# A four-block attention kernel: masked keys written by transfers, feature-major keys with DMA transposes, the causal triangle on VectorE, half-height numerators and a new instruction order

## The chip, the core and the metric

The kernel runs on one core of a Trainium2 chip. Five engines work side by side, each through its own instructions in order: TensorE (PE, matmuls; its weight loads are listed as PEld), VectorE (DVE), ScalarE (ACT), GpSimd (POOL) and SyncE (SP), which here issues nearly all transfers. Transfers themselves run on 16 DMA engines. The metric is the device time of one execution in microseconds; the kernel before takes 500.85 us (median of three runs, 499.58 to 501.59).

## The reference

Input is x of 2048 tokens by 512 features in bf16. Four blocks follow one another, A, B, A, B, with the same weights; each adds its result to x. There are 32 heads of 16 features.

```python
# block A, for each of 4 segments of 512 tokens
logits = einsum('bhqd,bhkd->bhqk', qs, ks) * scale + mask       # causal inside the segment
p = softmax(logits); a_dot = einsum('bhqk,bhkd->bhqd', p, vs)
pq = phi(qs)                                                    # t + 1 if t > 0, else exp(t)
a_mem = einsum('bhld,bhde->bhle', pq, M) / (einsum('bhld,bhd->bhl', pq, z) + 1e-06)
o = g * a_mem + (1.0 - g) * a_dot
M = M + einsum('bhld,bhle->bhde', phi(ks), vs);  z = z + sum over l of phi(ks)

# block B
pq = q @ w_phi;  pk = k @ w_phi                                 # per head
phi_q = concat(softmax(pq), softmax(-pq));  phi_k = concat(softmax(pk), softmax(-pk))
kv = einsum('bhsf,bhsd->bhfd', phi_k, v);  z = sum over s of phi_k
o = (phi_q @ kv) / (phi_q @ z + 1e-6)
```

Each block begins with a layer norm and ends with a projection `wo`.

## The kernel before, in words

All of x stays in on-chip memory as 16 tiles of 128 tokens. "Layer" 0 and 1 are the two pairs (A, B). Block A of a layer has 4 segments of 4 tiles; a segment's heads go in 4 groups of 8 heads (128 features).

- `a_proj(L, s)` projects a segment: per group the keys K, feature-major (features on partitions), are evacuated to `KT`; four DVE instructions (lines 641 to 645, `Km`) multiply it by a 0/1 column of `m4` into the masked key tile `KM` (pool `pQ`, six buffers), in which each score matmul finds the keys of one head with the other heads' rows at zero. Queries go to `QT`, values to `VT`, and `VS` is a copy with the halves of the partitions swapped, made by two SP transfers. `phi` makes the memory features; those of the keys are transposed by a DMA transpose and summed into `MS32`/`MSb`.
- `a_att(L, s, i)` is one tile of queries. For each group and each key tile j up to i, 8 score matmuls of 64 rows (two at a time, on the two halves of the array) fill one of two 1024-wide PSUM buffers `D`; ACT takes the exponential (1024 elements, or 768 for the diagonal tile, which goes to the pool `pE`); then small matmuls multiply the exponentials with `VT` and `VS` into two PSUM tiles. On the diagonal two more matmuls (`tri` and `two64`, lines 734 to 737) add -1e9 above the diagonal before the exponential. For s >= 1, lines 773 to 796 add the memory term tile by tile: five small matmuls for the denominators (`NMd`), a DVE reciprocal of 32, four matmuls for the numerators (`NM`), a DVE product and a DVE sum. `out_proj` transposes the result, projects it and adds it to x.
- `b_keys(L, c, parts)` handles one 512-token chunk of block B's keys, token-major: per tile a projection, two exponentials on ACT, two DVE sums over heads (line 887, `Zred`), a DVE reciprocal of 64 (line 895, `rZ`), the value projection scaled by it (line 869, `Vt`), and then 8 x 4 matmuls that sum keys times values (`KV`).
- `b_query(L, c)` projects queries, takes exponentials, gets the normalising sums with small matmuls (`Zq`), computes two weights, and per tile runs 8 matmuls of 128 x 128 (`N`, line 952) against the block-diagonal `Rkv`, a copy on ACT, a weighting on DVE, a sum and `out_proj`.

Nothing of the order of the work is decided at run time. Every operation is recorded in a graph with its dependencies; the string `ORDER` then gives, packed, the global sequence of the operations, the engine of each operation that can run on more than one, and the buffer of each tile. `place` reads it; `emit` writes each engine's instructions in that sequence and adds the semaphore waits. So the PE, ACT, DVE and SP queues interleave the stages in a fixed way: projections of segment s+1, keys of block B and attention of segment s are woven together. All matmuls through the helper `mm` carry line 325, exponentials line 331, evacuations line 339 (ACT) or 340 (DVE), transposes line 344.

Of the kernel before, what the change touches and what calls it, by code (L numbers as in the profile page):

```python
# [10 lines left out]
ALU = mybir.AluOpType  # L11
# [285 lines left out]
class Kernel:  # L297
# [78 lines left out]
    def alloc(self):  # L376
# [8 lines left out]
        self.eps32 = sb("eps32", [128, H], BF16)  # L385
        self.two64 = sb("two64", [128, 2, 64], BF16)
        self.tri = sb("tri", [128, 64], BF16)
        self.ones8 = sb("ones8", [128, 8], F32)
# [23 lines left out]
        self.pQ = pool("pQ", N_KM, [128, 4, 2, 2, 128], BF16, {}, ("KM",))  # L412
# [20 lines left out]
    def setup(self):  # L433
# [36 lines left out]
        for g in range(NG):  # L470
            load(lambda g=g: [(self.WB["o"][:, g, :], inp["B_wo"][g * 128:(g + 1) * 128, :].rearrange("(h d) o -> d h o", d=16))],
                 128, [R("WBo", g)])
# [18 lines left out]
        for hf in range(2):  # L491
            v(lambda e, hf=hf: e.tensor_copy(self.tri[64 * hf:64 * hf + 64, :], tw.t[64 * hf:64 * hf + 64, 64 * hf:64 * hf + 64]), 100,
              [tw], [R("tri", hf)])
        v(lambda e: e.memset(self.epsln[:], LN_EPS), 70, [], [R("epsln")])
        v(lambda e: e.memset(self.onesb[:], 1.0), 100, [], [R("onesb")])
        v(lambda e: e.memset(self.eps32[:], 1e-6 / 128.0), 80, [], [R("eps8")])
# [94 lines left out]
    def phi(self, ps, dst, src=None):  # L591
# [4 lines left out]
        if src is None:  # L596
            self.g.op({"dve": (602, lambda e: e.tensor_scalar(dst.t[:], ps.t[:, 0:512], 0.0, None, op0=ALU.max)),
                       "act": (478, lambda e: e.activation(dst.t[:], ps.t[:, 0:512], ACT.Relu))}, [ps[0]], [dst], label="phmax")
        else:
            v(lambda e: e.tensor_scalar(dst.t[:], src.t[:], 0.0, None, op0=ALU.max), 202, [src], [dst], label="phmax", port=True)  # L600
# [23 lines left out]
    def a_proj(self, L, s):  # L624
# [7 lines left out]
        for g in range(NG):  # L632
# [3 lines left out]
            KT = self.T(self.p1, "KT")  # L636
            KM = self.T(self.pQ, "KM")
            pk = self.T(self.p1, "phiKT") if s < 3 else None
            self.wproj(ps, 0, self.WA["k"], [R("WA", "k", g // 2)], g, xT, opens=[KT] + ([pk] if pk else []), label="K")
            self.evac(lambda KT=KT: KT.t[:], lambda ps=ps: ps.t[:, 0:512], 512, [ps[0]], [KT], label="Kev")  # L640
            for sl in range(4):
                fn = lambda e, KM=KM, KT=KT, sl=sl: e.tensor_scalar(  # L642
# [505 lines left out]
```

## Time and profile before

| | before |
|---|---|
| median of three runs | 500.85 us |
| lowest, highest | 499.58, 501.59 us |
| span of the profiled execution | 497.1 us |
| PE, DVE, ACT busy share | 94%, 88%, 89% |
| TensorE clock granted | 9 tenths or more in all 40 slices |
| transfers | 30.20 MB in 89377 packets |

The profile is of one execution; its own time is listed only as the span, from the first to the last instruction. Rows of the profile name the source line, the engine, the operation, the output and input tiles without buffer numbers, the shapes and the count; then busy time and mean duration of one instruction, then idle time of that engine just before and what ended it. Rows of the timeline begin with start and duration in us. Where an instruction overlaps the next, its duration is longer than the distance between the two starts.

### The profile page before, as it was taken

How to read it: one execution, taken by the hardware profiler on the slowest of the kernel's cores; microseconds unless marked ns; L12 is line 12 of the kernel's file. 1: busy time of each engine (PE TensorE's matmuls, PEld its weight loads, DVE VectorE, ACT ScalarE, POOL GpSimd, SP SyncE). 2: the span in 40 equal slices, each digit the busy share in tenths (PEclk: the TensorE clock that was granted, in tenths of full speed). 3: DMA queues.
4: the chain of work that ended last, by engine and by line, in shares of the span. 5: the costliest groups of instructions: out<-in, count | busy, mean ns of one | idle time of the engine just before them, and what ended most of it. 6: DMA issues, size and time to landing. Idle time of an engine off the chain costs nothing.

```text
span 497.1 us, 22749 instructions
## 1 busy us (share of the span) xinstructions
PE 469.4 (94%) x10186; PEld 299.8 (60%) x10282; DVE 438.1 (88%) x1115; ACT 440.9 (89%) x611; POOL 58.8 (12%) x142
## 2 busy tenths in 40 slices
PE   9989999999999989999999999999999999999896
PEld 4446665566676676557555665467566757656652
DVE  7989999998778969987999999999797899889885
ACT  3889999997999989489999999999999998966992
POOL 4512201000001101001220221010001011010000
PEclk9999999999999999999999999999999999999999
DMA  8986733211112031000243444321303112110155
GB/s 227 251 142 89 81 76 47 61 27 38 41 31 53 7 47 36 12 1 1 45 75 74 82 79 69 63 47 34 58 11 50 37 34 34 26 24 2 44 113 164
DMA packets 89377, 30.20 MB, mean 61 GB/s; under 512 B 75936, under 2 KB 89280, under 8 KB 89280
## 3 DMA queue, kind: packets, MB, share of 16 engines
q1 hardware_dynamic: 88928, 28.46, 30.2%
q8 instruction: 80, 1.31, 1.1%
q10 hardware_dynamic: 288, 0.26, 0.2%
q14 instruction: 17, 0.14, 0.1%
q0 software_dynamic: 64, 0.02, 0.1%
HBM read 6.32 MB, written 2.10 MB: 17 GB/s over the span
## 4 chain that ended last, share of the span: by engine, by line
PE 61%; ACT 24%; DVE 9%; issue 3%; DMA 2%; SPq 0%; POOL 0%
PE G L325 41%; PE D L325 18%; ACT p L331 16%; ACT pE L331 6%; DMA X<-in_A_x_dram 1%; DVE p L961 1%; DVE X L826 1%; DVE pS L887 1%; DMA pX<-p 1%; DVE stats L552 1%; PE G L808 1%; DVE WA_v L508 1%; DVE pQ L642 1%; DVE pT L869 0%; ACT WB_v L339 0%
## 5 line engine op out<-in xcount | busy, mean ns | idle before, releaser
L331 ACT ACTIVATE p<-D 128x1024 bf16<-128x1024 f32 x256 | 255.6, 1045 | 13.6 <-PE D L325 12.4
L325 PE MATMUL D<-pK,pQ 64*128 64x128 bf16 (+1 forms) x2560 | 112.3, 212 | 2.9 <-ACT pE L331 0.7
L331 ACT ACTIVATE pE<-D 128x768 bf16<-128x768 f32 x128 | 104.0, 840 | 9.8 <-PE D L325 9.0
L325 PEld LDWEIGHTS D<-pK,pQ 64*128 64x128 bf16 x2560 | 70.9, 94 | 54.9 <-ACT p L331 20.5
L325 PE MATMUL G<-pV,p 64*128 64x34 bf16 (+1 forms) x1632 | 78.9, 178 | 0.5 <-ACT pE L331 0.2
L331 ACT ACTIVATE p<-G 128x512 bf16<-128x512 f32 x112 | 69.0, 633 | 7.8 <-PE G L325 7.0
L325 PEld LDWEIGHTS G<-pV,p 64*128 64x128 bf16 (+1 forms) x1632 | 70.4, 93 | 7.3 <-issue 2.6
L325 PE MATMUL G<-pV,pE 64*128 64x34 bf16 x1024 | 73.0, 175 | 1.5 <-issue 1.5
L325 PE MATMUL G<-pW,pE 64*128 64x34 bf16 x1024 | 71.3, 175 | 0.6 <-issue 0.5
L325 PE MATMUL G<-pW,p 64*128 64x34 bf16 x1536 | 70.4, 176 | 0.8 <-issue 0.8
L325 PEld LDWEIGHTS G<-pW,p 64*128 64x128 bf16 x1536 | 63.8, 93 | 0.8 <-issue 0.4
L560 POOL TENSOR_SCALAR rstd<-mv 128x1 f32<-128x1 f32 x60 | 15.5, 261 | 379.6 <-DVE mv L553 379.6
L325 PEld LDWEIGHTS G<-pV,pE 64*128 64x128 bf16 x1024 | 53.3, 93 | 3.3 <-issue 3.2
L325 PEld LDWEIGHTS G<-pW,pE 64*128 64x128 bf16 x1024 | 50.5, 92 | 0.7 <-issue 0.7
L552 DVE BATCH_NORM_STATS2 stats<-X 128x6 f32<-128x512 bf16 x64 | 43.3, 682 | 3.1 <-DMA X<-in_A_x_dram 2.5
L642 DVE TENSOR_SCALAR pQ<-p,m 128x512 bf16<-128x512 bf16 x128 | 40.8, 340 | 2.6 <-PE D L325 1.6
L887 DVE TENSOR_REDUCE pS<-p 128x32 f32<-128x512 bf16 x64 | 41.7, 671 | 0.9 <-ACT p L331 0.6
L826 DVE TENSOR_TENSOR X<-X,G 128x512 bf16<-128x512 bf16 x48 | 32.5, 682 | 10.6 <-PE G L325 10.2
L869 DVE TENSOR_TENSOR pT<-G,pT 128x1024 bf16<-128x1024 f32 x30 | 36.2, 1212 | 2.3 <-PE G L325 1.9
L562 POOL TENSOR_TENSOR rstd<-rstd,mhalf 128x1 f32<-128x1 f32 x60 | 36.0, 605 | 3.7
L325 PE MATMUL D<-tri,two 64*128 64x256 bf16 x256 | 35.1, 270 | 0.0
L325 PE MATMUL G<-WA_v,pX 128*128 128x512 bf16 x128 | 32.9, 381 | 0.6 <-DVE WA_v L508 0.5
(118 smaller groups left out, 839.6 us busy)
## 6 DMA issues: line engine op xcount, KB each, us to landing
pW<-pV SPq DMA_DIRECT2D x16, 136.0 KB, 3.2
out_dram<-X SPq DMA_DIRECT2D x16, 128.0 KB, 1.8
X<-in_A_x_dram SPq DMA_DIRECT2D x3, 512.0 KB, 7.4
pX<-in_B_wqkv_dram SPq DMA_DIRECT2D x3, 512.0 KB, 7.3
p<-p SPq DMA_TRANSPOSE x76, 2.5
pX<-p SPq DMA_TRANSPOSE x54, 2.5
WA_k<-in_A_wk_dram SPq DMA_DIRECT2D x2, 256.0 KB, 7.5
WA_v<-in_A_wv_dram SPq DMA_DIRECT2D x1, 512.0 KB, 8.4
```

Source lines behind the costliest of these rows:

```text
L325: ins = e.matmul(out_ap, lhsT, rhs, start=st, stop=sp, tile_position=(basep(lhsT), basep(out_ap)))
L331: return self.g.op({"act": (dur, lambda e: e.activation(out_ap(), in_ap(), func, scale=scale))}, reads, writes, opens, label=label)
L508: fn = lambda e, dt=dt: e.tensor_tensor(self.WA["v"][:, dt, :].rearrange("p (h d) -> p h d", h=H), self.WA["v"][:, dt, :].rearrange("p (h ...
L552: v(lambda e: e.bn_stats(self.stats[:, t, :], self.X[:, t, :]), 602, [R("X", t)], [R("st", t)], label="bn")
L560: v(lambda e: e.tensor_scalar(rs, self.mv[:, t, 1:2], LN_EPS, None, op0=ALU.add), 170, [R("mv", t)], [R("rstd", t)], eng="pool", label="rstd")
L562: v(lambda e: e.tensor_tensor(rs, rs, self.mhalf[:], ALU.pow), 540, [R("rstd", t), R("mhalf")], [R("rstd", t)], eng="pool", label="rstd")
L642: fn = lambda e, KM=KM, KT=KT, sl=sl: e.tensor_scalar(KM.t[:, :, sl % 2, :, 64 * (sl // 2):64 * (sl // 2) + 64], KT.t[:].rearrange("p (j h ...
L808: ins = e.matmul(tp.t[:, k * 128:(k + 1) * 128], pair.t[:, sgn * 512 + k * 128:sgn * 512 + (k + 1) * 128], self.ident[:], start=sgn == 0, ...
L826: self.v(lambda e: e.tensor_tensor(self.X[:, t, :], self.X[:, t, :], ps.t[:, 0:512], ALU.add), 602, [R("X", t), ps[0]], [R("X", t)], label ...
L869: v(lambda e: e.tensor_tensor(dst(), ps.t[:, None, 0:512].to_broadcast([128, 2, 512]).rearrange("p s (g d h) -> p s g d h", g=NG, h=8), rz ...
L887: fn = lambda e, sgn=sgn, E=E, Z=Z: e.tensor_reduce(Z.t[:, sgn * 32:(sgn + 1) * 32], E.t[:, sgn * 512:(sgn + 1) * 512].rearrange("p (h d) ...
L961: v(lambda e, Ns=Ns, Tm=Tm, w=w, shape=shape: e.tensor_tensor(shape(Tm.t[:]), shape(Ns.t[:]), w(), ALU.mult), 600, [Ns, AB[0], AB[1]], [Tm ...
```

## The change

The changed kernel makes seven edits.

1. Masked keys: in segments 1 to 3 of both layers, the four DVE multiplications per group give way to transfers on SP that copy only the non-zero rows of `KT` into `KM`. Two groups share one `KT` and one `KM` tile (three buffers of double size in place of six); a pair takes four operations of two DMA copies each. A GpSimd memset zeroes one buffer at the start; the other two get their zeros from the first segment's multiplications, which remain there.
2. Causal triangle: the two `tri` matmuls stay only for the four tiles of layer 0, segment 0; in the other 28 tiles a DVE product of the exponentials with the 0/1 triangle `tri01` replaces them.
3. Memory term (`a_mem`): denominators of a whole segment at once, inverted by a logarithm and an exponential on ACT; numerators for two tiles at once, as 16 matmuls of 64 rows and 64 columns.
4. Keys of block B for chunks 0 to 2 (`b_keys_feat`): feature-major projection, two exponentials per group, a DMA transpose of each result, head sums by 32 small matmuls on PE (`Zk`), inverses by a logarithm and an exponential on ACT. The DVE sums and reciprocals of these chunks are gone. The summing matmuls (`kv_sum`) are as before.
5. `N` of block B: 16 matmuls of 64 rows and 64 columns for the 8 full-height ones, with the layout behind it (`Zq`, weights, halves, `wo`) permuted to fit.
6. Pools: `p1` from 20 to 16 buffers, `p2` from 18 to 20.
7. A new `ORDER` table. In the built programs ACT has 650 operations in place of 612, DVE 1027 in place of 1115, and SP 96 copies and 48 transposes more.

```diff
-        self.pQ = pool("pQ", N_KM, [128, 4, 2, 2, 128], BF16, {}, ("KM",))
+        self.pQ = pool("pQ", N_KM, [128, 2, 4, 2, 2, 128], BF16, {}, ("KM",))
...
+        self.pQ.init[N_KM - 1] = v(lambda e: e.memset(self.pQ.tensors[N_KM - 1][:], 0.0), 4400, [], [], eng=P, label="one")
...
-            for sl in range(4):
-                fn = lambda e, KM=KM, KT=KT, sl=sl: e.tensor_scalar(
-                    KM.t[:, :, sl % 2, :, 64 * (sl // 2):64 * (sl // 2) + 64], KT.t[:].rearrange("p (j h k) -> p j h k", j=4, h=2),
-                    self.m4[:, sl:sl + 1], None, op0=ALU.mult)
-                self.g.op({"dve": (262.0, fn)}, [KT, R("m4")], [KM[sl]], label="Km", port=True)
-            st["KM"].append(KM)
+            if (L, s) not in KM_DMA:
...
+            else:
+                if gg:
+                    for sl in range(4):
+                        rows = [slice(64 * hf + 16 * sl, 64 * hf + 16 * sl + 16) for hf in range(2)]
+                        self.dma(lambda KM=KM, KT=KT, sl=sl, rows=rows: [
+                            (KM.t[r, :, :, :, sl % 2, 64 * (sl // 2):64 * (sl // 2) + 64],
+                             KT.t[r, :].rearrange("p (g j x k) -> p g j x k", g=2, j=4, x=2)) for r in rows],
+                                 2, [KT[0], KT[1]], [KM[sl]], lat=2600.0, label="KmD")
+                st["KM"].append((KM, [KM[sl] for sl in range(4)]))
...
+    def a_mem(self, L, s, i):
...
+            self.mm(lambda: [(col(q, g), PQ[g].t[:, q * 128:(q + 1) * 128], self.MSb[mb][:, g, :, 16], True, True)
+                             for q in range(4) for g in range(NG)], [8] * 16, list(PQ) + ms, [mc], opens=[Rm], label="NMd")
+            self.g.op({"act": (158.0, lambda e: e.activation(Rm.t[:, 0:128], mc.t[:, 0:128], ACT.Ln, bias=self.eps6[:, 0:1]))},
+                      [mc, R("eps6")], [Rm], label="mln")
+            self.act(lambda: Rm.t[:, 128:256], lambda: Rm.t[:, 0:128], ACT.Exp, 128, [Rm], [Rm], scale=-1.0, psum=False, label="mln")
...
+        self.mm(lambda: [(NM.t[:, hf * 512 + (q - i) * 256 + g * 64:hf * 512 + (q - i) * 256 + g * 64 + 64], PQ[g].t[64 * hf:64 * hf + 64, q * 128:(q + 1) * 128],
+                          self.MSb[mb][64 * hf:64 * hf + 64, g, 4 * hf:4 * hf + 4, 0:16], True, True) for q in (i, i + 1) for g in range(NG) for hf in range(2)],
+                [], list(PQ) + ms, [NM], opens=[tmp], label="NM", rows=64, dur=240)
...
                     if not pem:
-                        for hf in range(2):
-                            pt4 = lambda PT=PT, hf=hf: PT.t[64 * hf:64 * hf + 64, :, 64:192].rearrange("p a (c e) -> p a c e", c=2)
-                            v(lambda e, pt4=pt4: e.affine_select(pt4(), pt4(), [[0, 4], [0, 2], [1, 64]], ALU.is_ge, 0.0, base=0, channel_multiplier=-1),
-                              587, [PT], [PT[hf]], eng="pool", label="mask")
+                        pt4 = lambda PT=PT: PT.t[:, :, 64:192].rearrange("p a (c e) -> p a c e", c=2)
+                        v(lambda e, pt4=pt4: e.tensor_tensor(pt4(), pt4(), self.tri01[:, None, None, :].to_broadcast([128, 4, 2, 64]), ALU.mult),
+                          335, [PT, R("tri01", 0), R("tri01", 1)], [PT], label="mask", port=True)
...
+    def b_keys_feat(self, L, c, part, xT):
...
+        for g in range(NG):
+            S = self.T(self.pG, "gen")
+            F = Fs[g] = self.T(self.p2, "EF")
+            E = Es[g] = self.T(self.p2, "ET")
+            self.wproj(S, 0, self.WB["k"], [R("WB", "k", i) for i in range(4)], g, xT, opens=[F], label="BK")
+            for sgn in range(2):
+                self.act(lambda sgn=sgn, F=F: F.t[:, sgn * 512:(sgn + 1) * 512], lambda S=S: S.t[:, 0:512], ACT.Exp, 512, [S[0]], [F[sgn]],
+                         scale=1.0 - 2.0 * sgn, label="kexp")
+                self.tr(lambda sgn=sgn, E=E: E.t[:, sgn * 512:(sgn + 1) * 512].rearrange("p (a b) -> p a b", a=4),
+                        lambda sgn=sgn, F=F: F.t[:, sgn * 512:(sgn + 1) * 512], [F[sgn]], [E[sgn]], label="ETr")
+        for g in range(NG):
+            self.mm(lambda g=g: [(zk()[:, tt, sgn, g * 8:g * 8 + 8], Fs[g].t[:, sgn * 512 + tt * 128:sgn * 512 + (tt + 1) * 128], self.H8b[:], True, True)
+                                 for sgn in range(2) for tt in range(4)], [8] * 8, [Fs[g][0], Fs[g][1], R("H8b")], [Z[g]], opens=[Z, lz], label="Zk")
+        self.act(lambda: lz.t[:], lambda: Z.t[:, 0:256], ACT.Ln, 256, [Z[g] for g in range(NG)], [lz], label="kln")
...
-            self.mm(lambda tt=tt, N=N: [(N.t[:, sgn * 512 + g * 128:sgn * 512 + (g + 1) * 128],
-                                         EQ[(g // 2, sgn)].t[:, (g % 2) * 512 + tt * 128:(g % 2) * 512 + (tt + 1) * 128],
-                                         self.Rkv[:, g * 2 + sgn, :, :], True, True) for sgn in range(2) for g in range(NG)],
+            self.mm(lambda tt=tt, N=N: [(N.t[:, hf * 512 + sgn * 256 + g * 64:hf * 512 + sgn * 256 + (g + 1) * 64],
+                                         EQ[(g // 2, sgn)].t[64 * hf:64 * hf + 64, (g % 2) * 512 + tt * 128:(g % 2) * 512 + (tt + 1) * 128],
+                                         self.Rkv[64 * hf:64 * hf + 64, g * 2 + sgn, :, 4 * hf:4 * hf + 4], True, True)
+                                        for sgn in range(2) for g in range(NG) for hf in range(2)],
...
-N_XT, N_KM, N_K1, N_K2, N_VT, N_SM, N_QT, N_PE = 5, 6, 20, 18, 5, 6, 6, 4
+N_XT, N_KM, N_K1, N_K2, N_VT, N_SM, N_QT, N_PE = 5, 3, 16, 20, 5, 6, 6, 4
...
-PMASK = {(L, t) for L in range(2) for t in range(16)}
+PMASK = {(0, t) for t in range(4)}
...
+FEAT = (0, 1, 2)
+KM_DMA = {(L, s) for L in range(2) for s in range(1, 4)}
```

More of the change, by code (lines that the diff above doesn't have):

```diff
@@ L738, in smm @@
                     return r
-                rd = [QT] + [KM[sl] for sl in range(4)] + ([R("two64"), R("tri", 0), R("tri", 1)] if dg and pem else [])
+                rd = [QT] + kres + ([R("two64"), R("tri", 0), R("tri", 1)] if dg and pem else [])
                 self.mm(smm, [], rd, [S], opens=[PT], label="Sd" if dg else "S", rows=64, dur=(176 + (110 if pem else 0)) if dg else 230)
@@ L966, in b_query @@
             if not pair:
[L967 to L968 removed]
+              v(lambda e, Tm=Tm, o=o: e.tensor_tensor(o.t[:].rearrange("p (a c) -> p a c", a=2), half(Tm, 0), half(Tm, 1), ALU.add), 335, [Tm], [o], label="nadd", port=True)
+            self.out_proj(t, o, [o], self.WB["o"], [R("WBo", g, hf) for g in range(NG) for hf in range(2)], store=store, res_pe=(L, t) in RES_PE, pair=Tm if pair else None)
     def build(self):
@@ L984, in build @@
                 gate = self.xnop[3]
[L985 removed]
+                for o in list(self.pV.init.values()) + list(self.pE.init.values()) + list(self.pQ.init.values()):
                     o.deps.add(gate)
```

300 lines of the change are left out of this document (167 added, 133 removed).

## The prediction

> **What bounds the kernel now.** I read the page first (span, busy shares, chain), then busy time by stage, then the waits, then single instructions on the timeline.
>
> ```profile
> span 497.1 us, 22749 instructions
> PE 469.4 (94%) x10186; PEld 299.8 (60%) x10282; DVE 438.1 (88%) x1115; ACT 440.9 (89%) x611; POOL 58.8 (12%) x142
> PE 61%; ACT 24%; DVE 9%; issue 3%; DMA 2%; SPq 0%; POOL 0%
> ```
>
> TensorE (PE) is busy 94% of the span and holds 61% of the chain that ended last; ScalarE (ACT) and VectorE (DVE) are close behind. The median of three runs is 500.85, so 500.85 - 497.1 = 3.75 us lie around the span; the page gives no own total for the profiled execution, so I work on the span and add 3.75.
>
> The stages below end where the last softmax exponential of a segment's attention ends: (layer 0, segment 0), (0,2), (1,0), (1,3), then the rest.
>
> ```profile
> core 0: us, PE busy (x) PEld busy (x) DVE busy (x) ACT busy (x) POOL busy (x), PEclk, DMA share, GB/s
> 0.00:65.00 65.00, 59.27 (x1195) 34.93 (x1205) 57.55 (x167) 53.29 (x82) 20.19 (x50) 1.00 0.79 155
> 65.00:154.00 89.00, 85.41 (x2237) 55.50 (x2252) 77.69 (x204) 84.45 (x114) 6.60 (x16) 1.00 0.23 44
> 154.00:305.00 151.00, 144.45 (x2840) 93.08 (x2872) 137.69 (x351) 136.36 (x193) 21.04 (x48) 1.00 0.25 45
> 305.00:437.00 132.00, 126.39 (x3366) 83.94 (x3387) 116.25 (x288) 125.06 (x164) 9.25 (x24) 1.00 0.23 40
> 437.00:497.10 60.10, 53.91 (x573) 32.38 (x578) 48.95 (x108) 41.79 (x63) 1.72 (x5) 1.00 0.29 71
> ```
>
> PE leads in every stage (96% in the three middle ones). In 65-154 and 305-437, almost pure attention, ACT is level with it (95%); in 154-305 and at the end, with layer B's queries, PE stands alone. DVE leads nowhere.
>
> ```profile
> PEld D L325 <- ACT p L331: 23.7, 62, 0.7
> ACT p L331 <- PE D L325: 12.4, 26, 3.8
> DVE X L826 <- PE G L325: 10.2, 16, 2.3
> ACT pE L331 <- PE D L325: 9.0, 18, 1.4
> DVE pS L369 <- PE G L325: 9.0, 13, 1.9
> ```
>
> ACT waits for PE's scores, DVE for PE's sums; PE's weight loads wait for ACT to free the two score buffers. No long wait for DVE stands there: what is taken off DVE alone is worth little, and PE's time is worth nearly its full amount.
>
> **PE, step by step.** A long matmul's busy time holds a pipeline tail, so I price by the distance from one start to the next.
>
> ```profile
> 59.63 0.81 PE L325 MATMUL G<-pX,WA_k 128*128 128x512 bf16 x3 [0.40 <-DVE WB_q L340]
> 60.37 0.40 PE L325 MATMUL D<-pK,pQ 64*128 64x128 bf16 x8
> 60.61 0.18 PE L325 MATMUL G<-pV,p 64*128 64x34 bf16 x1
> ...
> 62.37 0.27 PE L325 MATMUL D<-tri,two 64*128 64x256 bf16 x2
> 62.48 0.18 PE L325 MATMUL G<-pV,p 64*128 64x34 bf16 x1
> ...
> 230.13 1.03 PE L325 MATMUL G<-WB_o,p 128*128 128x512 bf16 x4
> 231.00 0.35 PE L325 MATMUL G<-Rz,p 128*128 128x16 bf16 x8
> 231.20 0.61 PE L325 MATMUL D<-Rkv,p 128*128 128x128 bf16 x8
> 231.64 0.61 PE L808 MATMUL G<-ident,p 128*128 128x128 bf16 x8
> L325 PE MATMUL D<-tri,two 64*128 64x256 bf16 x256 | 35.1, 270 | 0.0
> ```
>
> - Triangle off PE: the pair starts at 62.37, the next matmul at 62.48: 0.11 us. The mask stays on PE in 4 of 32 tiles, so 28 tiles x 4 groups = 112 pairs go: 112 x 0.11 = 12.3 us. The group's busy time is the upper bound: 35.1 x 112/128 = 30.7. I take 12.3, since pairs overlap their neighbours.
> - Numerators N: today 8 full-height matmuls take 231.64 - 231.20 = 0.44. The new 16 of 64 rows and 64 columns stream as many columns as the 8 score matmuls at 60.37, which run two at a time and take 60.61 - 60.37 = 0.24. Saved: 32 tiles x 0.20 = 6.4; nothing if the pairs do not overlap.
> - Memory numerators NM: today 4 matmuls a tile, 0.22 by the same row; new, 16 half-height ones for two tiles, 0.24. 24 x 0.22 - 12 x 0.24 = 2.4 saved.
> - Memory denominators: 24 x 5 small matmuls become 96. At (231.20 - 231.00)/8 = 0.025 each, 0.6 saved. New key sums Zk: 192 x 0.025 = 4.8 added.
> - Height changes: the last of the three 128x512 at 59.63 starts about two steps of (1.03 - 0.38)/3 = 0.216 later, at 60.06, and the 64-row matmul follows after 0.31 instead of 0.216: 0.095 us more. In the built order of both programs PE changes between 64 and 128 rows 318 times before and 360 after, mostly round N: 42 x 0.095 = 4.0 added.
>
> Sum on PE: -12.3 - 6.4 - 2.4 - 0.6 + 4.8 + 4.0 = -12.9 us.
>
> **DVE and ACT.**
>
> ```profile
> L642 DVE TENSOR_SCALAR pQ<-p,m 128x512 bf16<-128x512 bf16 x128 | 40.8, 340 | 2.6 <-PE D L325 1.6 <-ACT p L339 0.9
> L887 DVE TENSOR_REDUCE pS<-p 128x32 f32<-128x512 bf16 x64 | 41.7, 671 | 0.9 <-ACT p L331 0.6
> L369 DVE RECIPROCAL pT<-pS 128x64 bf16<-128x64 f32 x30 | 16.1, 540 | 0.1
> L369 DVE RECIPROCAL pS<-G 128x32 f32<-128x32 f32 x24 | 8.2, 342 | 0.2
> L794 DVE TENSOR_TENSOR p<-G,pS 128x512 bf16<-128x512 f32 x24 | 16.4, 685 | 3.3 <-PE G L325 2.8 <-issue 0.2
> L869 DVE TENSOR_TENSOR pT<-G,pT 128x1024 bf16<-128x1024 f32 x30 | 36.2, 1212 | 2.3 <-PE G L325 1.9
> L796 DVE TENSOR_TENSOR p<-p 128x512 bf16<-128x512 bf16 x24 | 10.0, 418 | 0.2
> L331 ACT ACTIVATE pS<-pS 128x128 f32<-128x128 f32 x16 | 5.0, 317 | 0.3
> ```
>
> DVE loses 96 of 128 key masks (40.8 x 96/128 = 30.6), 48 of 64 key reduces (31.3), 24 of 30 reciprocals of 64 (12.9) and all 24 of 32 (8.2); the memory product goes from 24 instructions (16.4) to 12 double ones like L869's (14.5). It gains 112 triangle products priced as L796: 112 x 0.417 = 46.7. Net -38, from 438 to 400, which off the chain I count as 2 us of shorter waits on the span (0 if the cover holds, 5 if half of the 9.0 of DVE pS is such queueing).
>
> ACT gains 30 small logarithms and exponentials for the key sums and 12 for the memory denominators, at most 42 x 0.31 = 13.0; three normalisations (0.8 each) and one 1.16 permutation leave it; the built order keeps as many 512-wide evacuations on it. Net +9.4, to 450.
>
> The triangle sits between exponential and weighted sum: in its tile PE waits 0.42 us later, more if DVE is in a 1.2 us instruction. Cover: other groups' scores and sums, which PE has ready. Without it, 112 x 0.42 = 47 us. I take none on the path.
>
> **Transfers.** Removed mask work returns as 96 copies of 16 partitions x 256 pieces (32 KB), and each feature-major key block needs 8 transposes, 48 in all, queued on SP.
>
> ```profile
> 42.53 0.60 SPq L677 DMA_DIRECT2D pW<-pV  x1
> 43.23 1.25 SPq L344 DMA_TRANSPOSE p<-p  x1
> pW<-pV SPq DMA_DIRECT2D x16, 136.0 KB, 3.2
> p<-p SPq DMA_TRANSPOSE x76, 2.5
> ```
>
> SP issues a copy of as many pieces in 0.60 and a transpose in 1.25: 96 x 0.60 + 48 x 1.25 = 118 us more on a queue that has 138 x 1.25 + 16 x 0.60 = 182 for transposes and swaps. Total share is harmless, the crowding is not: in the new order between the last exponentials of (0,1) and (0,2), SP has 24 transposes and 27 copies, 30 + 16 = 46 us, beside about 48 us of PE's work by the steps above. Behind SP's waiting instruction stand the transposes of attention outputs, whose projections PE waits for. Three key buffers hold pairs of groups, two a segment, so the second pair of a segment is written late: six batches, whose first score stands 0 to 8 us of PE's work after the batch's last copy in the order, against 3.2 for a landing. I take zero on the path; 0 to 3 us each.
>
> Sum: 497.1 - 12.9 - 2 = 482.2 on the span, with 3.75 **486 us**.
>
> **Rivals.**
> 1. *Late keys (slower).* Score matmuls wait at the six tight batches because SP is held up; behind them stands all of PE. Price: a batch issues in 8 x 0.60 and lands 3.2 later, 8.0 in all; 4 exposed each gives 24, so 482.2 + 24 + 3.75 = 510. It decides from 15/6 = 2.5 us a batch on. For it: the 46 of 48 us; against: (182 + 118)/486 leaves SP over a third of the span idle, and copies of a quarter of the bytes may land sooner. [...] No row of this trace shows a copy so small between two on-chip tiles.
> 2. *The triangle joins the chain.* A third of its 47 us shows, 16 us: 482 + 16 + 3.75 = 502, no change. For it: ACT-to-PE waits are already the commonest. Against: DVE has 12% idle and gets more.
> 3. *ACT holds the attention stages.* 20 of the 28 unmasked tiles lie in 65-154 and 305-437, where ACT is at 95%; their 8.8 us of the 12.3 are lost, and DVE's 2: 497.1 - 4.1 + 3.75 = 497.
> 4. *More.* PE's gain is nearer its busy time (12 of the 18 us between both bounds): 486 - 12 = 474.
>
> **How the numbers follow.** Forecast 0.50 (486), more 0.17 (474), ACT 0.13 (497), late keys 0.13 (510), triangle 0.07 (502). About 0.5% (2.5 us) is what a measurement tells from no change. Faster: 0.50 + 0.17 + 0.13 = 0.80; same 0.06 (the triangle's case, less its slower edge); slower 0.14. The forecast's own range is 477 (half of the extra triangle gain) to 495 (N and NM save nothing). The stated one goes from 471 to 505: rival 4 below, rivals 2 and 3 and the edge of rival 1 above.
>
> **What would show it.** PE's busy time near 456 and still first, DVE near 400, ACT near 450; the triangle rows gone but for 32 matmuls; N's 16 matmuls in 0.24 us plus 0.1 at each end; no wait of PE on a transfer over 5 us in all. Waits of D on a key-buffer transfer of 15 us or more mean rival 1; waits of the weighted sums on DVE's pE, rival 2; ACT at 97% in attention, rival 3. I am wrong in kind if PE's busy time falls by 13 and the span does not follow.

## The result and the profile after

| | before | after |
|---|---|---|
| median | 500.22 us (498.87 to 501.59, 4 runs) | 578.29 us (572.27 to 583.86, 4 runs) |
| ratio, 95% interval | 1 | 1.1502 (1.1425 to 1.158) |
| span of the profiled execution | 497.1 us | 577.4 us |

The change costs 78 us. Some executions of a kernel run at a lower granted clock and are slower (here 583.86 us at 0.936, the others at 0.950 to 0.952); ratios leave them out, medians do not. These are rows of the page of the kernel after; the third is the granted clock in 40 slices, the last the chain that ended last.

```profile
span 577.4 us, 23500 instructions
PE 478.2 (83%) x10490; PEld 295.1 (51%) x10578; DVE 413.1 (72%) x1027; ACT 450.2 (78%) x649; POOL 65.2 (11%) x145
PEclk9899889998899889999999889997799998899899
PE 50%; DMA 18%; DVE 12%; issue 7%; ACT 7%; SPq 3%; POOL 3%; ACTq 0%
```

No engine has become the bound. PE falls from 94% to 83% of the span, ACT from 89% to 78%, DVE from 88% to 72%: all wait for one another. Transfers go from 2% to 18% of the chain. The clock, full in every slice before, is at 7 or 8 tenths in 14 of 40; PE's busy time rises by 8.8 us (469.4 to 478.2), although the edits give it fewer columns to stream: at a lower clock the same matmuls are busy for longer. Eight score matmuls take 0.40 and 0.35 us at 68.45 and 69.07, with the clock at 1.00, and 0.51 and 0.66 at 72.45 and 72.94, with 0.50.

What PE waits for is in its waits: engine, line and tile; what ended the wait; then us in total, times, longest. Some 90 matmul records are missing from each of these two traces, so I read the weight loads (PEld), which are complete. First the kernel after:

```profile
PEld G L325 <- issue: 52.9, 90, 2.6
PEld D L325 <- issue: 31.3, 67, 1.2
PEld G L325 <- DMA p<-p: 24.6, 17, 4.4
PEld D L325 <- ACT p L331: 23.7, 50, 2.6
PEld G L325 <- DMA pX<-p: 13.1, 8, 3.6
```

The same view of the kernel before, where no wait on `p<-p` stands among its first seven rows:

```profile
PEld D L325 <- issue: 17.7, 42, 0.5
PEld G L325 <- issue: 9.8, 20, 1.6
```

Two things have grown. Waits that nothing in the profile explains ("issue") go from 27.5 to 84.2 us. Waits on DMA transposes, of attention outputs (`p<-p`) and of layer norms (`pX<-p`), come to 37.7 us. Waits for ACT's score buffers are what they were. Among the groups by line, the output projection shows it best, before and after:

```profile
L325 PE MATMUL G<-WA_o,p 128*128 128x512 bf16 x109 | 28.8, 379 | 2.8 <-issue 2.5 <-DVE p L796 0.2
```

```profile
L325 PE MATMUL G<-WA_o,p 128*128 128x512 bf16 x113 | 31.3, 392 | 19.4 <-DMA p<-p 18.0 <-issue 1.1
L789 DVE TENSOR_TENSOR pE<-pE,tri 128x512 bf16<-128x512 bf16 x112 | 45.2, 417 | 20.4 <-ACT pE L331 20.0
```

How such a wait comes about is seen on the timeline at one tile (layer 0, segment 2, tile 3). Columns: start, duration, engine, what, count; in brackets idle time before and its end. After:

```profile
195.38 0.19 PE L325 MATMUL G<-pV,pE 64*128 64x34 bf16 x1
...
195.62 0.37 DVE L369 RECIPROCAL pS<-G 128x16 f32<-128x16 f32 x2 [1.72 <-PE G L325]
...
196.70 0.43 DVE L828 TENSOR_TENSOR p<-p 128x512 bf16<-128x512 bf16 x1
...
197.16 1.20 SPq L344 DMA_TRANSPOSE p<-p  x1
...
198.04 0.78 PE L325 MATMUL D<-pK,pQ 64*128 64x128 bf16 x16
...
201.23 0.81 PE L325 MATMUL G<-WA_o,p 128*128 128x512 bf16 x3 [2.41 <-DMA p<-p]
```

The last weighted sum ends at 195.57; reciprocal, product, sum and transpose follow without a gap, and the projection starts 5.7 us later. In that time the order gives PE work until 198.82 only: then it stands for 2.41 us, and everything behind it too. Of the 5.7 us, 4.1 lie between the issue of the transpose (197.16) and the projection; the median transpose lands after 2.5 us. The same tile before:

```profile
155.28 0.17 PE L325 MATMUL G<-pV,pE 64*128 64x34 bf16 x1
...
158.56 1.19 SPq L344 DMA_TRANSPOSE p<-p  x1
...
163.17 1.04 PE L325 MATMUL G<-WA_o,p 128*128 128x512 bf16 x4
```

The order puts 7.7 us of PE's work between the sum (155.45) and the projection, and nothing waits for the transpose. The tile is no exception. By the durations written in the two kernels, the order before has a median of 7.2 us of PE's work between an attention tile's last weighted sum and its projection, the order after 5.25, over the 30 tiles whose result goes through a DMA transpose; under 4 us stand 1 of 30 before and 8 of 30 after. That does not yet show the cause: SP's queue, the traffic or the instructions themselves could be late as well. That is what the experiments tell apart.

### The profile page after: what moved, and what is told of

Read it like the earlier page. It is cut to its first block, busy times and chain, and to the rows that moved or that the text cites. A ratio compares the mean times of both kernels' runs of the same rounds, so it can differ in the third digit from the quotient of the medians.

```text
span 577.4 us, 23500 instructions
## 1 busy us (share of the span) xinstructions
PE 478.2 (83%) x10490; PEld 295.1 (51%) x10578; DVE 413.1 (72%) x1027; ACT 450.2 (78%) x649; POOL 65.2 (11%) x145
## 3 DMA queue, kind: packets, MB, share of 16 engines
q8 instruction: 83, 1.36, 1.1%
## 4 chain that ended last, share of the span: by engine, by line
PE 50%; DMA 18%; DVE 12%; issue 7%; ACT 7%; SPq 3%; POOL 3%; ACTq 0%
PE G L325 35%; PE D L325 14%; DMA p<-p 8%; DMA pX<-p 8%; ACT p L331 5%; SPq L344 2%; DVE p L580 2%; DVE X L858 2%; DVE stats L559 1%; DMA WA_v<-in_A_wv_dram 1%; ACT pE L331 1%; DVE pT L901 1%; DVE pE L789 1%; DVE p L820 1%; DVE p L1036 1%
## 5 line engine op out<-in xcount | busy, mean ns | idle before, releaser
L331 ACT ACTIVATE pE<-D 128x768 bf16<-128x768 f32 x128 | 102.6, 824 | 30.4 <-PE D L325 29.9
L325 PE MATMUL D<-pK,pQ 64*128 64x128 bf16 (+1 forms) x2560 | 115.7, 218 | 9.5 <-issue 4.0
L325 PEld LDWEIGHTS D<-pK,pQ 64*128 64x128 bf16 x2560 | 73.2, 97 | 62.8 <-issue 27.3
L325 PE MATMUL G<-pV,p 64*128 64x34 bf16 (+1 forms) x1632 | 81.2, 180 | 8.0 <-issue 5.9
L331 ACT ACTIVATE p<-G 128x512 bf16<-128x512 f32 x112 | 66.0, 612 | 22.8 <-PE G L325 19.0
L325 PE MATMUL G<-pV,pE 64*128 64x34 bf16 x1024 | 74.9, 176 | 7.0 <-issue 5.3
L325 PEld LDWEIGHTS G<-pV,p 64*128 64x128 bf16 (+1 forms) x1632 | 70.8, 94 | 16.5 <-issue 11.9
L789 DVE TENSOR_TENSOR pE<-pE,tri 128x512 bf16<-128x512 bf16 x112 | 45.2, 417 | 20.4 <-ACT pE L331 20.0
L325 PE MATMUL G<-WA_o,p 128*128 128x512 bf16 x113 | 31.3, 392 | 19.4 <-DMA p<-p 18.0
L369 DVE RECIPROCAL pS<-G 128x16 f32<-128x16 f32 x64 | 13.6, 236 | 35.3 <-PE G L325 35.2
L325 PE MATMUL G<-pX,WA_k 128*128 128x512 bf16 x113 | 31.1, 402 | 8.8 <-DMA pX<-p 5.4
```

Of the source, the lines that this page charges most:

```text
L325: ins = e.matmul(out_ap, lhsT, rhs, start=st, stop=sp, tile_position=(basep(lhsT), basep(out_ap)))
L331: return self.g.op({"act": (dur, lambda e: e.activation(out_ap(), in_ap(), func, scale=scale))}, reads, writes, opens, label=label)
L369: return e.reciprocal(o, i)
L789: v(lambda e, pt4=pt4: e.tensor_tensor(pt4(), pt4(), self.tri01[:, None, None, :].to_broadcast([128, 4, 2, 64]), ALU.mult), 335, [PT, R("t ...
```

## The experiments

The theories, in the order in which they were formed: T1, the new transfers hold SP's queue, and the transposes behind them come late; T2, their traffic delays the fetching of PE's instructions; T2a, PE's small instructions arrive at a limited rate whatever the traffic, and the new order makes them denser; T3, each short stall is followed by a half clock, which multiplies it; T5, the new order itself leaves no work between a result and its use. Ratios are against the kernel before, measured beside each run (499.5 to 504.6 us).

**The new transfers, out or elsewhere.** Four kernels keep the order of the kernel after. The first leaves out the 96 copies:

```diff
-                if gg:
+                if gg and KM_COPY:
...
+KM_COPY = False
```

> The changed kernel with its order kept and the 96 masked-key copies of segments 1 to 3 left out, so the scores there read the masks left in the buffers by the segment before. After: 578 us. Theory 1 (SyncE's queue is full, so the transposes that TensorE waits for are issued late): the copies hold the queue 96 x 0.61 = 59 us of the 118 us that the change added, so about half of the 78 us lost comes back: 535 to 550. Theory 2 (the traffic itself: the 52,000 extra packets on the 16 DMA engines starve TensorE's instruction fetch and slow the transposes): the copies are nearly all of the extra packets, so most comes back: under 520. Late keys (the forecast's first rival): the scores wait for no copy any more, but they waited 1.2 us in all before, so by the trace 577. Triangle on VectorE or the order table: no change, 575 to 580.

The second leaves out the 48 transposes:

```diff
-                self.tr(lambda sgn=sgn, E=E: E.t[:, sgn * 512:(sgn + 1) * 512].rearrange("p (a b) -> p a b", a=4),
-                        lambda sgn=sgn, F=F: F.t[:, sgn * 512:(sgn + 1) * 512], [F[sgn]], [E[sgn]], label="ETr")
...
-        return (lambda sl, tt: Es[sl // 2].t[:, (sl % 2) * 512 + tt * 128:(sl % 2) * 512 + (tt + 1) * 128], Vts,
+        return (lambda sl, tt: self.WB["k"][:, sl // 2, tt * 128:(tt + 1) * 128], Vts,
```

> The changed kernel with its order kept and the 48 DMA transposes of layer B's key exponentials left out; the key-value sums read a weight tile of the same shape in their place. Theory 1 (SyncE's queue): the transposes hold the queue 48 x 1.21 = 58 us, about half of what was added, all of it in the stages of segments 0 to 2: 530 to 550. Theory 2 (traffic): these transposes are few packets beside the copies; 565 or more. Triangle or order table: 575 to 580.

The third has both edits:

> Both left out: the 96 copies and the 48 transposes; order kept, the other changes (triangle on VectorE, 64-row numerators) stay. Theories 1 and 2 alike: all of the loss that comes from the DMAs comes back, 485 to 500, with a granted clock of 1.00 and TensorE's waits on the layer-norm and output transposes back to a few us. If more than 520 is left, the cause lies in the order table, the triangle or the numerators.

The fourth issues the copies from GpSimd's queue:

```diff
-                                 2, [KT[0], KT[1]], [KM[sl]], lat=2600.0, label="KmD")
+                                 2, [KT[0], KT[1]], [KM[sl]], lat=2600.0, label="KmD", eng="pool")
```

> The changed kernel, same order and the same 96 copies, but issued from GpSimd's queue and not from SyncE's. Nothing is left out. Theory 1 (SyncE's queue): the same gain as leaving the copies out, 535 to 550, since SyncE is rid of 59 us. Theory 2 (traffic): the packets are the same, so 570 to 585. Where GpSimd is slower at issuing, the scores come to wait for the masked keys: waits of D on the key buffer above 10 us, and a time that can go over 580.

| | median us | ratio, 95% interval |
|---|---|---|
| copies out | 571.22 | 1.1308 (1.1238 to 1.1378) |
| transposes out | 565.28 | 1.1226 (1.1186 to 1.1266) |
| both out | 561.23 | 1.1042 (1.0981 to 1.1103) |
| copies from GpSimd | 591.0 | 1.1722 (1.1667 to 1.1777) |

Without any new transfer 52 of 75 us remain by the ratios (1.1042 and 1.1502 of 500): T1 and T2 together explain some 23. Neither accounts for the whole, which would have meant 550 or less with one set out and 500 or less with both. The waits of the kernel with both out:

```profile
PEld G L325 <- issue: 40.2, 64, 2.5
PEld D L325 <- issue: 25.0, 53, 1.5
...
PEld G L325 <- DMA p<-p: 20.5, 19, 2.8
PEld G L325 <- DMA pX<-p: 12.3, 6, 5.2
```

Both kinds of waits stay, although SP has no more transposes or copies than in the kernel before. Issued from GpSimd's queue, the copies cost 11 us more than from SP's by the ratios, 13 by the medians. This run doesn't price a freer SP by itself, since the copies also land later there, after 3.6 us in place of 2.3; but with the copies out altogether the waits on `p<-p` fall only from 24.6 to 20.8 us.

**What "issue" is.** A kernel with nothing but PE: four stretches of 1536 64-row matmuls of 34 columns with their weight loads, and four 512-column matmuls after every 512, 128, 64 or 32 of them. All inputs are zeros set on the chip.

```diff
+        def pv(n):
...
+            self.mm(items, [], [R("E"), R("V")], PV, label="PV", rows=64, dur=n * 25.5)
...
+        for m in DENSE:
+            for k in range(1536 // m):
+                pv(m)
+                wide()
...
+DENSE = (512, 128, 64, 32)
```

> Not the reference's computation: TensorE alone runs a stream of 64-row matmuls of 34 columns as in the weighted sums, in four stretches of 1536 each, with four 512-column matmuls put in after every 512, 128, 64 and 32 of them; no transfer runs beside it and no instruction waits; the output is written as zeros. In the changed kernel 17 gaps inside such sums, 25 us in all, end 2.3 to 2.9 us after a 16 KB fetch of instructions begins (16 KB is 256 instructions, 128 pairs of weight load and matmul). Theory 2a (instructions are fetched too slowly for a dense stream, whatever the transfers): gaps of 1 to 2 us about once in 128 pairs in the first stretch, fewer in the second, none in the last, where 128 pairs take over 5 us. Theory 2 (transfers delay the fetch): no gap over 0.5 us anywhere, since none run.

Its timeline in the first stretch, PE only, and one line of its list of transfer queues (packets, MB, share):

```profile
26.06 1.77 PE L325 MATMUL G<-WA_k,WA_q 64*128 64x34 bf16 x128 [1.28 <-issue]
30.06 2.11 PE L325 MATMUL G<-WA_k,WA_q 64*128 64x34 bf16 x128 [2.23 <-issue]
...
41.52 2.00 PE L325 MATMUL G<-WA_k,WA_q 64*128 64x34 bf16 x128 [2.04 <-issue]
45.25 2.10 PE L325 MATMUL G<-WA_k,WA_q 64*128 64x34 bf16 x128 [1.73 <-issue]
```

```profile
q8 instruction: 51, 0.84, 1.7%
```

PE waits for nothing in this kernel, and still stops before each 128 matmuls for 1.3 to 2.2 us; from one start to the next it takes 4.00 and 3.73 us. The instruction queue moves 0.84 MB / 51 = 16.5 KB at a time. From 9.84 to 216 us, nearly the whole run, PE has 6503 weight loads, each with its matmul; an estimate from these counts is 2 x 6503/51 = 255 instructions to a piece, which agrees with the 128 weight loads and 128 matmuls between two stops. In the kernel after it moves 1.36 MB / 83 = 16.4 KB at a time, and with the 0.14 MB of a second instruction queue 1.50 MB for 23500 instructions: by these counts 257 to a piece. So, by this reading, PE's instructions arrive in pieces, here some 128 load-and-matmul pairs in 3.7 to 4.0 us. Windows of the same kernel, with the clock (PEclk) and the share of the transfer engines in the two columns before the last:

```profile
core 0: us, PE busy (x) PEld busy (x) DVE busy (x) POOL busy (x), PEclk, DMA share, GB/s
25.00:28.41 3.41, 1.77 (x128) 1.67 (x128) 0.00 (x0) 0.00 (x0) 1.00 0.03 5
28.41:38.65 10.24, 6.88 (x330) 5.55 (x332) 0.00 (x0) 0.00 (x0) 0.50 0.02 3
72.00:97.00 25.00, 18.43 (x917) 14.17 (x923) 0.00 (x0) 0.00 (x0) 1.00 0.02 5
97.00:140.00 43.00, 38.26 (x1471) 26.10 (x1492) 0.00 (x0) 0.00 (x0) 1.00 0.02 5
```

The transfer engines are all but idle (0.02), so the stops need no traffic: T2a stands. Whether traffic lengthens them too (T2) is left open; with both sets of transfers out, "issue" falls from 84.2 to 65.2 us. And a window with PE busy for 1.77 of 3.41 us is followed by 10.24 us at half clock, as T3 has it. With four 512-column matmuls after every 128 or 64 (third and fourth row, from 72 us on), the clock is full, and 128 take 25.0 x 128/917 = 3.5 and 43.0 x 128/1471 = 3.7 us, against 10.24 x 128/330 = 4.0 at half clock: over these windows the rate changes little, though in the last PE's own work fills 89% of the time.

The kernel after has the same sequence between 66 and 77 us:

```profile
core 0: us, PE busy (x) PEld busy (x) DVE busy (x) ACT busy (x) POOL busy (x), PEclk, DMA share, GB/s
66.45:69.86 3.41, 1.59 (x106) 1.50 (x99) 1.40 (x4) 1.52 (x3) 0.00 (x0) 1.00 0.23 46
69.86:76.69 6.83, 4.92 (x94) 2.79 (x87) 2.39 (x10) 4.05 (x7) 1.63 (x5) 0.50 0.17 26
```

The mean clock of the run was 0.95, against 1.00 before: if PE had work throughout, 0.05 x 577 = 29 us at most of the loss are this echo of stalls. How much of the 84 us of "issue" is arrival is not shown; the stops that could be tied to such a piece (recorded above) came to 25 us.

**The triangle back on PE**, in the order of the kernel after:

```diff
-PMASK = {(0, t) for t in range(4)}
+PMASK = {(L, t) for L in range(2) for t in range(16)}
```

> The changed kernel with the triangle given back to TensorE (two matmuls a tile, 112 tiles) and taken from VectorE, order of the rest kept. By the forecast's sum this costs TensorE 12 us, so 590 if TensorE's work still set the time. Theory 5 (the changed order itself leaves TensorE idle: what it waits for is placed too close behind what makes it): TensorE has 80 us of idle time and most of the 12 us goes into it, 572 to 586. Forecast's rival 2 (triangle in the chain): faster, 560 or less.

573.06 us, 1.1392 (1.1329 to 1.1455): 5 us less than with the triangle on DVE, though PE gets 112 pairs of matmuls back. The intervals of the two overlap. Only the exchange as a whole is measured, and it is a small part of the 78 at most.

**The order alone.** Only the string `ORDER` is replaced, by another sequence of the same operations on the same engines, with other buffers for the tiles. Each was searched for with the durations of the traces; they differ in what else was counted, and each search gave one order. The first search already counted transposes at 2.5 us (up to 1.6 more in one case of five), no more than 128 pairs in 3.7 us, and the lower clock after stretches with little work; but it took a result as ready 0.06 us after its instruction gave way to the next. One kernel uses it for the operations of after, one for those of before:

> The changed kernel, every instruction of it and nothing else, in another order: a new table found by a search that counts a DMA transpose at 2.5 us and up to 1.6 us more in one case of five, instructions for 128 pairs of weight load and matmul at most every 3.7 us, and the lower TensorE clock after a stretch with under 60% work. Theory 5 (the loss is the order's: no slack behind the transposes, streams of short matmuls denser than their instructions arrive, and the lower clock that follows the stalls): 478 to 510, granted clock back at 1.00, gaps inside the sums gone, TensorE's waits for transposes under 10 us. Theory 1 or 2 (the 144 new DMAs): they are all there, so 560 or more. The triangle: also all there, 570.

> The kernel before, same instructions, with an order from the same search: what the search itself is worth. Theory 5 gives less here than in the changed kernel, since the order of before has slack already (its idle TensorE time is 28 us): 475 to 500. If it gains as much as the changed kernel, the order of the changed kernel is not what sets it apart.

565.1 us, 1.1309 (1.123 to 1.1389), and 527.76 us, 1.0555 (1.0497 to 1.0614). The first gains 13 us, where 478 to 510 were expected under T5: by itself it spoke against T5. The second says more: the same work as the kernel before, in another order, costs 28 us, where 475 to 500 were expected. Worse still with transposes taken to land in 1.45 us, and neither arrival nor clock counted:

> The kernel before, same instructions, with an order from the same search, which now counts a transpose at 1.45 us and knows neither of the instructions' arrival nor of the clock. None of the change's parts is in it. Theory 5: an order that is the better by such costs is the worse on the chip, 510 to 540, with gaps inside the sums and half-clock stretches as in the changed kernel. If order hardly matters: 480 to 500.

545.36 us, 1.0916 (1.0855 to 1.0976), a loss of 45 us with no other change. Its waits are of the same kinds as those of after:

```profile
PEld G L325 <- issue: 21.6, 46, 2.4
PEld D L325 <- issue: 20.9, 47, 1.0
PEld G L325 <- DMA p<-p: 14.3, 16, 2.7
```

So the order can cost this much, and the first search had missed something. The next one counted beside landing and arrival what the traces show from a result to its reader, some 0.1 us behind an ACT or DVE instruction and 0.3 to 0.4 behind a PE one, and that one transpose in eight holds SP for 2.0 us (41 of the 324 in the traces of before and after for over 1.9 us; the median is 1.27). With the operations of after:

> The changed kernel, all its instructions and DMAs, in a second new order. The first search counted a result as ready 60 ns after its instruction gave way to the next; the traces show 120 to 170 ns for ScalarE, 85 to 125 for VectorE and 300 to 400 for TensorE, and a transpose that holds SyncE for 2.0 us in one case of eight. The search now counts these. Theory 5 (the loss is the order's): 500 to 530, well under the 565 of the first try, with TensorE's idle time under 45 us. If the change's DMAs or operations themselves cost what was lost: 560 or more again.

532.07 us (530.79 to 534.05), 1.0604 (1.0525 to 1.0682). The same instructions and transfers, 46 us faster: so much of the loss is the order's. Counted as above, its median is 6.0 us of PE's work between last sum and projection, where the order of after has 5.25. Two more searches count one of the two parts each, the landing and result times without the arrival limit, then the limit without these times:

> The changed kernel, all instructions, in an order whose search counts the latencies as the traces show them (transposes, DMAs, ends of instructions) but nothing of the arrival of instructions. With 578 for the change's own order and 532 for the order whose search counted both, this tells the two apart. If late operands (no slack behind transposes) are the larger part of what the order lost: 535 to 555, with gaps of 15 us or more left inside the sums. If the arrival of instructions is: 560 or more.

> The other half: an order whose search counts the arrival of instructions (128 pairs in 3.65 us) but takes a transpose to land 1.45 us after its start and a result to be ready as soon as its engine goes on. If late operands are the larger part: 560 to 590, with the gaps inside the sums gone and TensorE's waits for transposes and for ScalarE as long as in the changed kernel or longer. If the arrival of instructions is: 530 to 550.

547.3 us, 1.0934 (1.0898 to 1.097), and 579.7 us, 1.162 (1.1543 to 1.1696).

| us of PEld's waits (line 325) | median us | issue, G + D | DMA p<-p |
|---|---|---|---|
| after | 578.29 | 84.2 | 24.6 |
| first search: landing and arrival | 565.1 | 57.8 | 12.3 |
| landing and result times counted | 547.3 | 66.4 | 8.4 |
| arrival limit counted | 579.7 | 57.0 | 28.5 |
| all three counted | 532.07 | 40.3 | 8.5 |

The rows behind the last four lines of the table, in this sequence:

```profile
PEld G L325 <- issue: 31.9, 74, 2.7
PEld D L325 <- issue: 25.9, 51, 2.0
...
PEld G L325 <- DMA p<-p: 12.3, 13, 2.8
```

```profile
PEld G L325 <- issue: 39.8, 69, 2.4
...
PEld D L325 <- issue: 26.6, 58, 2.5
...
PEld G L325 <- DMA p<-p: 8.4, 7, 2.8
```

```profile
PEld D L325 <- issue: 29.4, 55, 1.6
...
PEld G L325 <- DMA p<-p: 28.5, 21, 3.5
PEld G L325 <- issue: 27.6, 65, 2.0
```

```profile
PEld D L325 <- issue: 21.8, 52, 1.3
PEld G L325 <- issue: 18.5, 37, 2.0
...
PEld G L325 <- DMA p<-p: 8.5, 6, 2.9
```

Each search lowers the wait that it counts, but none removes it. Landing and result times together are worth 31 us (578 to 547; 28 by the ratios). The arrival limit is worth 15 on top (547 to 532; 17 by the ratios) and nothing alone, where PE waits for transposes as long as before. By an estimate, those 15 us may have come mostly through the clock: it was granted at 0.953 in the one profile and 0.980 in the other, and what is lacking to 1.00 makes 0.047 x 547 = 26 and 0.020 x 529 = 11 us.

Landing and result times were not parted. The first search counts landing and arrival and gains 13 us only, although both its waits are well under those of after; so the waits do not add up to the time, and landing times alone cannot be given the 31. What the two searches with the larger gains share is the result times. With one order for each search, some of each difference may also be chance.

**What is left, in the better order.** Both sets of transfers out, with the edits shown above:

> The 532 us order with the 96 copies and the 48 transposes of layer B's key exponentials left out, all else and the order kept (the sums read a weight tile of the same shape, the masks are those of the segment before). In the change's own order leaving them out gave 17 us. Theory 1 as the smaller part (SyncE's queue): 10 to 20 us again, 512 to 522. If the order hid them: 527 or more. If they are what is left of the loss: 500 to 505.

517.97 us, 1.036 (1.0319 to 1.04): the transfers cost 14 us here, 12 by the ratios. Only the copies undone, DVE multiplying all masks again, in an order of its own from the same search:

```diff
-KM_DMA = {(L, s) for L in range(2) for s in range(1, 4)}
+KM_DMA = set()
```

> A version that may beat the changed kernel: the changed kernel without the masked-key copies (VectorE writes the masks as before, 96 operations of 0.26 us more than the changed kernel), in an order from the second search. SyncE loses 59 us of holds, VectorE gets 25 us. If SyncE's queue is worth 7 us or more, as leaving the copies out was: 515 to 530. No slower than 532 in any case where VectorE is not in the chain.

525.29 us, 1.0502 (1.0466 to 1.0537): 7 us less than with the copies, but the order differs too, so the copies' share of the 14 us is not shown by it. DVE has room for the masks, and this is the best version of the changed kernel that I found. It does not reach the kernel before. The triangle once more, on PE in the better order:

> The 532 us order with the triangle given back to TensorE and taken from VectorE, order of the rest kept. The forecast priced the triangle at 12 us of TensorE's time; in the change's own order giving it back made the kernel 5 us faster. If TensorE's work sets more of the time in the better order: 532 to 544. If VectorE's mask stands in the chain in any order: under 528.

532.83 us (530.62 to 534.6), 1.0689 (1.0637 to 1.0741), beside 532.07 with it on DVE. The range of each holds the median of the other: 112 pairs of matmuls on PE or off make no difference that these runs can tell.

**One part alone.** The kernel before with the 64-row numerators and the layout that they need, its order kept:

```diff
-                                         self.Rkv[:, g * 2 + sgn, :, :], True, True) for sgn in range(2) for g in range(NG)],
...
+                                         self.Rkv[64 * hf:64 * hf + 64, g * 2 + sgn, :, 4 * hf:4 * hf + 4], True, True)
```

> One part alone: the kernel before with the 64-row numerators of the change (sixteen matmuls of 64 columns for eight of 128, output weights laid out to match), everything else and the order as before. The forecast's sum: 32 x 0.20 = 6.4 us less on TensorE, less some height changes: 493 to 498. If TensorE's time is not what bounds the end: 499 to 502.

504.52 us, 1.005 (1.0009 to 1.009): slightly slower, where 493 to 498 were expected. Two rows of its timeline show the sixteen matmuls and what follows them:

```profile
237.04 0.41 PE L325 MATMUL D<-Rkv,p 64*128 64x64 bf16 x16
237.39 1.04 PE L325 MATMUL G<-WA_v,pX 128*128 128x512 bf16 x4
```

From one start to the next they take 0.35 us: the 0.24 of the prediction and one change of height, as priced. PE's busy time falls from 469.4 to 468.4 us; the span goes from 497.1 to 500.2. The same in the order of the better search:

> The kernel before with the 64-row numerators, in an order from the second search. Theory 5: the search's costs now agree with the chip, so this is no slower than before and perhaps faster than both kernels: 482 to 500. If it comes out at 515 or more, the search still misses a cost, and what it says of the changed kernel's order is a lower bound only.

509.62 us, 1.0149 (1.0078 to 1.022). Here the search loses 5 us to the order of the kernel before; some of what is left of the 78 us may be its own shortfall.

## Why the prediction was wrong

It said 486 us and faster; the time is 578. It is wrong in kind, much as its last sentence puts it: PE's work fell and the span did not follow. PE's busy time itself rose, by 8.8 us, but it holds the lower clock. An estimate without that comes from the runs whose PE records are complete, as busy time less what the clock lacked over the span: with the operations of before 495.2 - 0.016 x 528.1 = 487 and 496.6 - 0.016 x 540.5 = 488 us (the two searched orders), with those of after between 490.2 - 0.047 x 546.9 = 465 (landing and result times counted) and 499.0 - 0.043 x 562.9 = 475 (the first search's). That is 12 to 24 us less work, and the sum had 12.9: its part on PE held.

- *"PE's time is worth nearly its full amount"* is the step that failed, and with it the sum, which has no term for edit 7, the new `ORDER`. The 94% of PE were read as a property of the work. They are a property of the order: the same operations of before in another order lose 28 or 45 us, those of after gain 46. Of the 78 us, 46 go with the order alone, 14 with the new transfers, and 18 remain.
- *Transfers at zero on the path.* Wrong by 12 us in the better order and 23 in the change's own, but not by the rival's mechanism. The prediction named the right place ("Behind SP's waiting instruction stand the transposes of attention outputs, whose projections PE waits for") and put no price on it. Its bound, 3 us for each of six key batches, was drawn for the keys.
- *Late keys* (rival 1) did not happen. The view of the key buffers lists ACT, DVE and "issue" as what ended the idle time before their readers, and no transfer. The copies take SP what was priced, and land as fast as the row of the larger swaps:

```profile
L348 SPq DMA_DIRECT2D pQ<-p x96: 585/612/1980, 59.0 to 465.9; - x96
pQ<-p SPq DMA_DIRECT2D x96, 32.0 KB, 2.3
pW<-pV SPq DMA_DIRECT2D x16, 136.0 KB, 2.6
```

  The first row gives the shortest, median and longest hold of SP in ns: 612 against the 0.60 us taken. A copy of 32 KB lands after 2.3 us, one of 136 KB after 2.6: a quarter of the bytes landed 0.3 us sooner, where a landing in proportion to bytes would be 2.6 x 32/136 = 0.6 us.
- *The triangle.* Its price on DVE was right (0.417 us each, 45.2 in all against 46.7). In the better order the exchange as a whole gains and costs nothing that these runs can tell. So the 12.3 us taken off PE did not shorten the kernel: either they gained nothing, or the product on the path took them back. "None on the path" is thus neither shown nor refuted.
- *N and the height changes.* Expected from this part alone: 32 x 0.20 = 6.4 saved, and in that kernel's built order 318 changes of height become 370, 52 x 0.095 = 4.9 added, so 1.5 us faster. PE's busy time fell by 1.0, so the term was about right as work on PE. The time went up by 0.1% to 0.9%, 0.5 to 4.5 us: here too a little less work on PE did not make a shorter span; why is open.
- *DVE and ACT.* ACT was right (450.2 against 450). DVE fell to 413, not 400. Neither bounds anything: rival 3 wanted ACT at 97% in the attention stages; it is at 78% of the span. Rival 2's sign is absent, PE's weight loads for the sums wait for DVE's `pE` for 1.0 us in all; and rival 4, a larger gain, is far off.

What stays open is the last 18 us (518 to 500), in a kernel with neither set of new transfers and, by the prediction's steps, some 13 us less work on PE. The 5 us that the search loses with the operations of before may be part of it; the key sums, logarithms, the paired memory term and the new buffer counts were not tried alone.

## What to carry to other kernels

A static order is part of the change: before an engine's busy time is taken as the price, look at how much of its own work the new order puts between each result and its reader, and compare that with the landing time of a transpose (2.5 us in the median, 4.9 at most in the kernel after) and with the whole chain (5.7 us here). Count the tenths of a microsecond from each result to its reader as well; both orders that gained most did. An engine at 94% is at the mercy of that order: less work for it did not shorten this kernel, a better order of the same work gained 46 us. Wide matmuls among small ones kept PE busier and the clock up: in the kernel of matmuls alone, with four 512-column ones after every 512 small ones (9.84 to 58 us) PE was busy for 65% of the time at a mean clock of 0.68, with four after every 64 (97 to 140 us) for 89% at 1.00.

## What was not expected of the hardware

- In the kernel of matmuls alone the instruction queue moves 16.5 KB at a time (255 instructions by the estimate above), and a dense run of 64-row, 34-column matmuls gets 128 load-and-matmul pairs in 3.73 us, although 128 run in 1.77 at full clock. The profile shows the stop as "issue" (1.3 to 2.2 us), with the transfer engines at 0.02.
- The clock is at half for 6.83 us (the kernel after) or 10.24 us (matmuls alone) after a window of 3.41 us with PE busy for about half of it (1.59 and 1.77 us; in the kernel of matmuls alone also after one with 2.03 us, from 11.35 us on). These half-clock stretches (0.50) are two and three times 3.41 us. No gap in these windows was longer than 2.23 us: 2.03 of 3.41 us busy (60%) did not keep the clock, 18.43 of 25 us (74%, from 72 us on) went with 1.00.
- 32 KB copies between on-chip tiles landed after 3.6 us from GpSimd's queue and after 2.3 from SP's; the kernel took 591.0 us against 578.3.
